# A static instruction order replanned: bank turns, two-row-half score products, work moved between VectorE, GpSimdE and ScalarE, and identity products in early pauses

## The chip, the cores and the metric

One core of one Trainium2 chip. The metric is the device time of one execution in microseconds (us). Engines are called by the profile's names: PE (TensorE's products), DVE (VectorE), ACT (ScalarE), POOL (GpSimdE) and SP (which issues the transfers here).

## The reference

Three stages in float32, one after the other:

```python
# 1: attention, 2 batches x 8 heads x 768 positions x 64; a row keeps 8 global and 96 local keys
scores = q @ k.T / 8 - slope[h] * dist;  a = softmax(where(keep, scores, -1e9));  x = a @ v
# 2: 1536 tokens, 512 -> 2048 -> 512
h = x @ w_in
g = (a0 + a1*h + a2*h**2 + a3*h**3) / (1 + |b0|*|h| + |b1|*h**2 + 1e-6);  x = g @ w_out
# 3: 512 -> 1024 -> 512
h = x @ w_in2;  s = h * softmax(h);  out = (layernorm(s) * g_ln) @ w_out2
```

## The kernel before

**The plan.** `record` (line 300) writes the whole program down as small operations, each with an engine, a planned duration (`lat`), the time after which its engine is free (`occ`) and what it reads and writes. `Plan.run` (202) then simulates the engines at build time: whenever an engine is free it takes the operation whose due time (worked back from the end, less a `lead`) is earliest, and the instructions are issued in just that order. At run time each engine executes its list in order and waits on semaphores. So a wrong planned duration costs nothing by itself, but puts an instruction at a place in its queue where it may hold up what stands behind it. `lock=True` marks operations that want the memory port which DVE and POOL share.

**Attention.** 48 units, each 128 queries of two heads; 128 keys for the first tile of a batch (n=1), else 256 (n=2). `u_load` (390) brings q/k and v by SP. `u_front` (398): scores on PE (lines 405-406, both heads into two halves of one PSUM bank; q is padded with zeros, so that each product runs over all 128 rows), score plus bias and row maximum on DVE (411), exp on ACT (418), reciprocal on DVE (423-424), scaling by it on POOL (429). `u_back` (438): transposes on PE (446), copy out on ACT (458), the product with v on PE (453, the two heads in two 64-column halves of the array), results split in a high and a low part on ACT (460) and DVE (82).

**Second stage.** Four blocks of 384 tokens, 64 steps in five segments, of 8, 16, 16, 16 and 8 steps. The attention of block 0 (12 units) stands ahead of step 0; that of block 1 is recorded in steps 0 to 7, of block 2 in 8 to 22, of block 3 in 24 to 38 (`UW`). A step makes one 128x384 h by 12 products (`h_mm`, lines 574-580), g by a chain of ACT and DVE operations that all use h's bank (`e_ops`, 600-619, its last one on POOL), and three steps later 9 products into the y banks (`y_mm`, 665-671).

**Weights.** 48 pieces, of 512 KB as 64-bit floats, are loaded by SP (485) and rebuilt as float32 by integer operations (`w_conv`): ACT scales (509), POOL reduces the high word to its sign (526, "signs"), DVE shifts and joins (530, 518). The form without "signs" exists in the code as `bits`, two DVE operations (513-514), but `ZS = range(48)` selects "signs" for all. `w_split` makes a high part (ACT, 548) and a low one (POOL, 549, shown as L82). Pieces 0 to 31 are of stage 2, 32 to 47 of stage 3.

**Third stage.** 12 tiles: transposes (731), 24 products into two banks (750-752, tag "h2"), the softmax and norm chain on DVE and ACT (772-794), transposes of its result (812, "lT"), their copies (820, 82), 24 products (834-836, "o"), output.

**Bias.** `bias_pair` (367): eight DVE operations that stand between the first units' maxima.

Of the kernel before, what the change touches and what calls it, by code (L numbers as in the profile page):

```python
# [30 lines left out]
UW = {1: (0, 7), 2: (8, 15), 3: (24, 15)}  # L31
# [3 lines left out]
M2 = (41, 22)  # L35

ZS = range(48)
# [3 lines left out]
WLEAD = 2.0  # L41


SLOW = (5.0, 1.2)
# [82 lines left out]
class Plan:  # L127
# [4 lines left out]
    SEM = 0.05  # L132
# [54 lines left out]

    def settle(self, n):
# [13 lines left out]
    def run(self, emit=True):  # L202
        self.deadlines()
        self.pools = {p: [(0.0, s) for s in sl] for p, sl in self.slots.items()}
        for v in {v for o in self.ops for v in o.vals}:
            v.left, v.free = len(v.users), 0.0
# [18 lines left out]
        while left:  # L225
            best = None
            for e, l in ready.items():
                c = []
                for o in l:
                    t = max(o.t0, at[e])  # L230
                    ok = True
                    need = {}
                    for v in o.new:
# [3 lines left out]
                        need[v.pool] = need.get(v.pool, 0) + 1  # L237
                        fr = self.pools[v.pool]
                        if self.line[v.line][x][0] is not v or len(fr) < need[v.pool]:
                            ok = False  # L240
                            break
                        t = max(t, sorted(fr)[need[v.pool] - 1][0])
                    if ok:
                        if o.lock:
                            t = max(t, port)
                        c.append((t, o))
# [18 lines left out]
            at[e] = t + o.occ  # L265
            o.end = t + o.lat
            if o.lock:
                port = t + o.occ
            if e == "SP":
                dma = max(dma, at[e]) + o.move  # L270
                o.end = dma + o.lat
            for v in o.vals:
                v.left -= 1
# [14 lines left out]
def fast_path(tc, const, qkv, w_in, w_out, w2_in, w2_out, coef, g_sb, nv, ident, out):  # L288
# [3 lines left out]
    plan.settle(ROUNDS)  # L292
    with tc.manual_schedule():
        plan.run()
# [5 lines left out]
def record(tc, es, const, qkv, w_in, w_out, w2_in, w2_out, coef, g_sb, nv, ident, out):  # L300
# [29 lines left out]
    op = P.op  # L330
# [22 lines left out]
    def bias_keep():  # L353
# [26 lines left out]
    xs = {}  # L380
# [9 lines left out]
    def u_load(u):  # L390
        u.qk, u.v = Val("qk"), Val("v")
        w = 256 + u.w
        uop("SP", 2.0, lambda: sync.dma_start(out=qkt[u.qk.slot][:, 0:w], in_=qkv[u.t, u.p, :, 0:w]), occ=0.4,
            new=[u.qk], move=0.8, tag="ld")
        uop("SP", 2.0, lambda: sync.dma_start(out=vt[u.v.slot][:, 0:u.w], in_=qkv[u.t, u.p, :, w:w + u.w]), occ=0.4,
            new=[u.v], move=0.4, tag="ld")

    def u_front(u, bank):
        u.s, u.e, u.st = Val(bank), Val("e"), Val("st")
        w, b0, n = u.w, 0 if u.first else 8, u.w // 128  # L400

        def qk():
            a = qkt[u.qk.slot]
            for h in range(2):
                pe.matmul(out=pb[:, u.s.slot, h * 256:h * 256 + w], lhsT=a[:, h * 128:(h + 1) * 128],  # L405
                          rhs=a[:, 256:256 + w], start=True, stop=True)

        def smax():
            e, st = et[u.e.slot], stt[u.st.slot]
            for h in range(2):  # L410
                dve.tensor_tensor_reduce(out=e[:, h, 0:w], in0=pb[:, u.s.slot, h * 256:h * 256 + w],  # L411
# [778 lines left out]
```

## Time and profile before

| | us |
|---|---|
| median of 3 runs (568.31 to 568.39) | 568.36 |
| the profiled execution's own time | 569.23 |
| its span, first to last instruction | 567.4 |
| PE busy in the span | 529.6 (93%) |
| DVE busy | 429.2 (76%) |
| ACT busy | 390.2 (69%) |
| POOL busy | 223.9 (39%) |

The profiled execution took 0.87 us more than the median of the runs. Busy time is the union of an engine's instructions; a share of the whole span hides that the stages differ, so the stages are read one by one. PE's ends are modelled, so that a short pause between two of its products can count as busy.

### The profile page before, as it was taken

How to read it: one execution, taken by the hardware profiler on the slowest of the kernel's cores; microseconds unless marked ns; L12 is line 12 of the kernel's file. 1: busy time of each engine (PE TensorE's matmuls, PEld its weight loads, DVE VectorE, ACT ScalarE, POOL GpSimd, SP SyncE). 2: the span in 40 equal slices, each digit the busy share in tenths (PEclk: the TensorE clock that was granted, in tenths of full speed). 3: DMA queues.
4: the chain of work that ended last, by engine and by line, in shares of the span. 5: the costliest groups of instructions: out<-in, count | busy, mean ns of one | idle time of the engine just before them, and what ended most of it. 6: DMA issues, size and time to landing. Idle time of an engine off the chain costs nothing.

```text
span 567.4 us, 8749 instructions
## 1 busy us (share of the span) xinstructions
PE 529.6 (93%) x2808; PEld 437.8 (77%) x2808; DVE 429.2 (76%) x1045; ACT 390.2 (69%) x903; POOL 223.9 (39%) x278
## 2 busy tenths in 40 slices
PE   4899998999989899999999989998999999999985
PEld 2567887878877688888887877877878888888865
DVE  6777888998999997677679999889866555555540
ACT  4788888898988888777788887877634444433331
POOL 3675456546677743332335563756400000000000
PEclk9999999999999999999999999999999999999989
DMA  7779255533444443110043230233001111000001
GB/s 247 244 259 324 89 167 161 165 102 94 130 160 152 134 133 114 36 58 26 2 149 130 75 115 34 76 111 104 25 21 39 40 54 37 22 35 20 18 20 43
DMA packets 28278, 56.24 MB, mean 99 GB/s; under 512 B 3520, under 2 KB 11968, under 8 KB 28224
## 3 DMA queue, kind: packets, MB, share of 16 engines
q1 hardware_dynamic: 28080, 55.59, 30.0%
q8 instruction: 24, 0.39, 0.3%
q14 instruction: 30, 0.25, 0.1%
q10 hardware_dynamic: 144, 0.00, 0.0%
HBM read 47.72 MB, written 7.86 MB: 98 GB/s over the span
## 4 chain that ended last, share of the span: by engine, by line
PE 51%; DVE 27%; ACT 15%; issue 4%; POOL 1%; DMA 1%; ACTq 0%; SPq 0%; POOLq 0%; DVEq 0%
PE pb L834 4%; PE pb L836 4%; PE pb L835 4%; PE pb L405 4%; PE pb L750 4%; PE pb L752 4%; PE pb L751 4%; DVE t L615 3%; DVE t L604 3%; DVE t L602 3%; PE pb L453 3%; PE pb L574 3%; PE pb L665 3%; PE pb L580 3%; DVE t L613 3%
## 5 line engine op out<-in xcount | busy, mean ns | idle before, releaser
L82 POOL TENSOR_TENSOR g<-t,g 128x384 fp32r<-128x384 f32 x64 | 69.4, 1084 | 79.9 <-ACT g L617 74.2
L574 PE MATMUL pb<-x,w 128*128 128x384 f32 x256 | 90.0, 352 | 5.4 <-DVE t L607 5.2
L576 PE MATMUL pb<-x,w 128*128 128x384 f32 x256 | 86.2, 337 | 0.0
L665 PE MATMUL pb<-w,g 128*128 128x512 f32 x192 | 78.3, 408 | 7.4 <-ACT g L617 6.3
L429 POOL TENSOR_SCALAR e<-e,st 128x256 f32<-128x256 f32 (+1 forms) x96 | 47.3, 505 | 75.0 <-DVE st L424 56.1
L666 PE MATMUL pb<-w,g 128*128 128x512 f32 x192 | 76.2, 397 | 0.0
L82 POOL TENSOR_TENSOR w<-wst,w 128x512 fp32r<-128x512 f32 x48 | 64.7, 1354 | 18.8 <-ACT w L548 16.2
L574 PEld LDWEIGHTS pb<-x,w 128*128 128x128 f32 x256 | 48.2, 188 | 14.0 <-DVE t L607 10.7
L580 PE MATMUL pb<-x,w 128*128 128x384 f32 x256 | 57.5, 346 | 0.0
L671 PE MATMUL pb<-w,g 128*128 128x512 f32 x192 | 57.2, 406 | 0.0
L405 PE MATMUL pb<-qk 128*128 128x256 f32 (+1 forms) x192 | 50.0, 392 | 6.7 <-DMA qk<-in_qkv 5.4
L602 DVE TENSOR_TENSOR t<-t,pb 128x384 f32<-128x384 f32 x64 | 35.1, 548 | 22.3 <-ACT t L603 20.8
L418 ACT ACTIVATE e<-e,st 128x256 f32<-128x256 f32 (+1 forms) x96 | 46.3, 486 | 5.3 <-DVE st L411 5.1
L665 PEld LDWEIGHTS pb<-w,g 128*128 128x128 f32 x192 | 36.3, 189 | 17.4 <-ACT g L617 9.3
L580 PEld LDWEIGHTS pb<-x,w 128*128 128x128 f32 x256 | 44.7, 188 | 6.2 <-issue 2.4
L576 PEld LDWEIGHTS pb<-x,w 128*128 128x128 f32 x256 | 48.3, 189 | 1.3
L405 PEld LDWEIGHTS pb<-qk 128*128 128x128 f32 x192 | 35.4, 208 | 12.9 <-DMA qk<-in_qkv 5.4
L606 ACT ACTIVATE pb<-pb 128x384 f32<-128x384 f32 x64 | 30.4, 476 | 20.9 <-DVE t L604 20.6
L600 ACT ACTIVATE t<-pb,coef 128x384 f32<-128x384 f32 x64 | 42.6, 666 | 2.6 <-PE pb L580 1.6
L617 ACT CAST g<-t 128x384 fp32r<-128x384 f32 x64 | 32.7, 512 | 16.9 <-DVE t L615 10.6
L607 DVE SCALAR_TENSOR_TENSOR t<-pb,coef,t 128x384 f32<-128x384 f32 x64 | 39.2, 612 | 6.8 <-ACT pb L606 6.1
L615 DVE SCALAR_TENSOR_TENSOR t<-t,coef,t 128x384 f32<-128x384 f32 x64 | 42.7, 667 | 0.7
(106 smaller groups left out, 1261.6 us busy)
## 6 DMA issues: line engine op xcount, KB each, us to landing
wst<-in_w_in SPq DMA_DIRECT2D x24, 512.0 KB, 4.3
wst<-in_w_out SPq DMA_DIRECT2D x24, 512.0 KB, 4.1
qk<-in_qkv SPq DMA_DIRECT2D x40, 256.0 KB, 3.2
v<-in_qkv SPq DMA_DIRECT2D x40, 128.0 KB, 2.5
y_d<-y SPq DMA_DIRECT2D x12, 256.0 KB, 2.7
y<-y_d SPq DMA_DIRECT2D x12, 256.0 KB, 2.6
out<-wst SPq DMA_DIRECT2D x11, 256.0 KB, 2.0
qk<-in_qkv SPq DMA_DIRECT2D x8, 192.0 KB, 3.3
```

The lines of the kernel that those rows point to most:

```text
L82: eng.tensor_tensor(out=out, in0=a, in1=hi.bitcast(F32), op=ALU.subtract)
L405: pe.matmul(out=pb[:, u.s.slot, h * 256:h * 256 + w], lhsT=a[:, h * 128:(h + 1) * 128], rhs=a[:, 256:256 + w], start=True, stop=True)
L418: act.activation(out=e[:, h, 0:w], in_=e[:, h, 0:w], func=AF.Exp, scale=-1.0, bias=st[:, h:h + 1], accum_out=st[:, 2 + 2 * h:3 + 2 * h])
L429: pool.tensor_scalar(out=e[:, h, 0:w], in0=e[:, h, 0:w], scalar1=st[:, 6 + h:7 + h], scalar2=0.0, op0=ALU.mult, op1=ALU.add)
L574: pe.matmul(out=pb[:, g.h.slot, 0:n], lhsT=wt[wh.slot][:, cs[p]], rhs=xt[x[p][0].slot][:, 0:n], start=(p == 0), stop=False)
L576: pe.matmul(out=pb[:, g.h.slot, 0:n], lhsT=wt[wl.slot][:, cs[p]], rhs=xt[x[p][0].slot][:, 0:n], start=False, stop=False)
L580: pe.matmul(out=pb[:, g.h.slot, 0:n], lhsT=wt[wh.slot][:, cs[p]], rhs=xt[x[p][1].slot][:, 0:n], start=False, stop=(p == 3))
L602: op("DVE", 0.14 + 0.41 * k, lambda: dve.tensor_tensor(out=T(g.c), in0=T(g.c), in1=h(), op=ALU.mult), r=[g.h], w=[g.c], tag="ch")
L615: op("DVE", 0.15 + 0.41 * k, lambda: stt_(out=T(g.c), in0=T(g.c), scalar=coef[:, 0:1], in1=T(g.b), op0=ALU.add, op1=ALU.mult), r=[g.b], w= ...
L665: pe.matmul(out=pb[:, y[i].slot, :], lhsT=gt[g.gh.slot][:, c], rhs=wt[wh.slot], start=g.first, stop=False)
L666: pe.matmul(out=pb[:, y[i].slot, :], lhsT=gt[g.gh.slot][:, c], rhs=wt[wl.slot], start=False, stop=False)
L671: pe.matmul(out=pb[:, y[i].slot, :], lhsT=gt[g.gl.slot][:, c], rhs=wt[wh.slot], start=False, stop=g.last)
```

## The change

- `Plan.run`: an operation on a PSUM bank may start only when the last operation on that bank, if it was another engine's, has ended; waits for the shared port lengthen the waiting operation instead of putting it back; an operation that needs two buffers of a pool can claim them. Planned durations, occupancies and start times are changed, and a table `LEADS` moves the due times of operations by tag.
- Scores of blocks 0 and 3 are made over 64 rows per head instead of 128 (`START = ('hh',)`, `TWO = (3,)`), into two banks instead of two halves of one.
- The scaling of 19 units (`NDVE`), the low part of 6 weights (`WDVE`) and 22 of the 48 "signs" (`ZS`, replaced by a second DVE operation) go from POOL to DVE. The eight bias operations go from DVE to ACT, with one DVE operation more ahead of them.
- Weights 16 to 31 are recorded over steps 8 to 22 instead of 6 to 14, those of stage 3 over 17 steps instead of 22; a load waits for the last h product recorded before it (`after`).
- In the first 30 planned microseconds, where PE is planned to pause, products of the identity with itself are put into an unused bank (`fill`).

```diff
-UW = {1: (0, 7), 2: (8, 15), 3: (24, 15)}
+UW = {1: (0, 7), 2: (8, 15), 3: (25, 14)}
-M2 = (41, 22)
-ZS = range(48)
+WS = (8, 14)
+M2 = (41, 17)
+ZS = (2, 4, 6, 8, 10, 12, 15, 17, 18, 20, 22, 24, 26, 28, 30, 32, 33, 34, 35, 36, 38, 40, 42, 44, 46, 47)
-SLOW = (5.0, 1.2)
+SLOW = (5.0, 0)
+START = ('hh',)
+TWO = (3,)
+NDVE, WDVE = (3, 4, 5, 6, 7, 8, 9, 10, 11, 14, 15, 36, 38, 39, 40, 41, 42, 44, 46), (11, 20, 31, 42, 44, 45)
+LEADS = {"o": -35.2, "ld": 41.4, "h2": 1.9, "norm": -0.8, "ex": -9.6, "wg": -18.1, "q": 0.2, "xcp": 0.6, "wld": -0.8, "yev": 9.0, "bias": -2.2, "ln": -1.0, "gl": -7.5, "yT": -12.1, "abs": -0.9, "wbits": -0.1, "pv": 0.0, "ch2": -0.5, "n3": 1.3, "lT": -8.0, "wlo": 0.5, "sq": -5.0, "tre": 10.0, "n2": -1.1, "xh": -0.2, "whi": 2.5, "xl": -0.7, "wzs": -1.6, "y": -0.4}
+BEGIN = {"PE": 2.0, "ACT": 5.0, "DVE": 3.4, "POOL": 1.0, "SP": 1.6, "X": 0.0}
+BANKS = ("h", "s", "p", "y0", "y1", "y2")
+FILL = (30.0, 0.45, 0.25)
...
+                    for v in o.vals:
+                        if v.pool in BANKS and v.last is not None and v.last.eng != e:
+                            t = max(t, v.last.end + self.SEM)
...
-            at[e] = t + o.occ
-            o.end = t + o.lat
+            wait = max(0.0, port - t - self.PORT) if o.lock else 0.0
+            at[e] = t + o.occ + wait
+            o.end = t + o.lat + wait
...
+                if e == "PE" and fill and t < FILL[0]:
+                    spare = [b for p in ("y2", "y1", "y0", "p") for f, b in self.pools[p] if f <= idle and b not in [v.slot for v in o.vals if v.pool in BANKS]]
+                    fill(int((t - idle - 0.1) / FILL[2 if idle > BEGIN["PE"] else 1]), spare)
...
+    def fill(n, spare):
+        for _ in range(n if spare else 0):
+            nc.tensor.matmul(out=plan.pb[:, spare[0], 0:128], lhsT=ident, rhs=ident, start=True, stop=True)
...
-        dve.tensor_scalar(out=kp, in0=kp, scalar1=-1.0, scalar2=-MASK, op0=ALU.add, op1=ALU.mult)
+        dve.tensor_scalar(out=kp, in0=kp, scalar1=-1.0, scalar2=MASK * 256, op0=ALU.add, op1=ALU.mult)
+        dve.tensor_tensor(out=dz, in0=dz, in1=kp, op=ALU.add)
     def bias_pair(p):
         for h in (2 * p, 2 * p + 1):
-            dve.scalar_tensor_tensor(out=bt[h], in0=dz, scalar=-8.0 * SLOPE[h], in1=kp, op0=ALU.mult, op1=ALU.add)
+            act.mul(bt[h], dz, -8.0 * SLOPE[h])
...
+        two, ndve = len(bank) == 2, u.k in NDVE
...
+        def score(h):
+            return pb[:, u.s[h].slot, 0:w] if two else pb[:, u.s[0].slot, h * 256:h * 256 + w]
...
-                pe.matmul(out=pb[:, u.s.slot, h * 256:h * 256 + w], lhsT=a[:, h * 128:(h + 1) * 128],
-                          rhs=a[:, 256:256 + w], start=True, stop=True)
+                r = slice(h * 64, (h + 1) * 64) if two else slice(0, 128)
+                pe.matmul(out=score(h), lhsT=a[r, h * 128:(h + 1) * 128], rhs=a[r, 256:256 + w], start=True, stop=True)
...
-                pool.tensor_scalar(out=e[:, h, 0:w], in0=e[:, h, 0:w], scalar1=st[:, 6 + h:7 + h],
-                                   scalar2=0.0, op0=ALU.mult, op1=ALU.add)
+                (dve if ndve else pool).tensor_scalar(out=e[:, h, 0:w], in0=e[:, h, 0:w], scalar1=st[:, 6 + h:7 + h],
+                                                      scalar2=0.0, op0=ALU.mult, op1=ALU.add)
...
-        op("POOL", 1.27, lambda: minus(nc, pool, wt[lo.slot], src(), wt[hi.slot]), r=[st, hi], w=[lo], lock=True, lead=WLEAD, tag="wlo")
+        if nlo[0] - 1 in WDVE:
+            op("DVE", 0.68, lambda: minus(nc, dve, wt[lo.slot], src(), wt[hi.slot]), r=[st, hi], w=[lo], lock=True, lead=WLEAD, tag="wlo")
...
-            w_make(wseq[made[0]])
+            w_make(wseq[made[0]], [gs[-1].op] if gs else [])
...
-            make_to(2 * s + 4)
+            make_to(min(2 * s + 4, max(2 * SEGS[0][2], 2 * SEGS[0][2] + (s - WS[0]) * (32 - 2 * SEGS[0][2]) // WS[1])))
...
-            w_make(w2seq[made2])
+            w_make(w2seq[made2], [gs[-1].op])
```

## Rows read from the trace of the kernel before

**Rows 1.** Busy time by stretch: us of the stretch, its length, then for each engine busy us (instructions), the granted clock of PE, the share of the DMA engines and GB/s. Block 0's attention; steps 0 to 23; steps 24 to 39; steps 40 to 63 and the first tile of stage 3; the end.
```profile
0.00:45.20 45.20, 32.81 (x183) 22.36 (x184) 32.95 (x142) 31.22 (x98) 27.09 (x51) 0.96 0.75 247
45.20:190.00 144.80, 137.92 (x801) 114.05 (x800) 131.38 (x328) 126.55 (x313) 87.72 (x109) 0.99 0.48 156
190.00:287.40 97.40, 96.67 (x550) 81.04 (x550) 74.68 (x196) 76.99 (x184) 38.33 (x49) 1.00 0.21 62
287.40:416.40 129.00, 120.21 (x576) 102.21 (x575) 115.20 (x202) 100.55 (x199) 70.80 (x70) 1.00 0.27 90
...
543.40:567.40 24.00, 15.19 (x89) 12.96 (x87) 4.33 (x10) 4.78 (x12) 0.00 (x0) 0.88 0.11 37
```

**Rows 2.** Waits over the span: who waited, for whom, us in total, times, longest. Operations 602 and 603 read the same h bank and share no other tile; 600, 603 and 606 are ACT's, 602, 604 and 607 DVE's.
```profile
DVE t L602 <- ACT t L603: 20.8, 20, 2.5
DVE t L604 <- ACT t L603: 3.4, 6, 0.7
SPq L485 <- POOL w L82: 85.2, 29, 9.7
```

**Rows 3.** The same view for 190 to 287 us (first row) and for 287 to 416 us (the others).
```profile
DVE t L602 <- ACT t L603: 15.4, 11, 2.5
...
PE pb L574 <- DVE t L607: 4.0, 6, 1.2
DVE t L602 <- ACT t L603: 2.8, 5, 0.9
```

**Rows 4.** Timeline of DVE: the same operations where they met no POOL operation, and where they did.
```profile
31.43 0.17 DVE L423 TENSOR_SCALAR st<-st 128x2 f32<-128x2 f32 x1
163.32 0.55 DVE L611 SCALAR_TENSOR_TENSOR t<-t,t 128x384 f32<-128x384 f32 x1
165.12 0.92 DVE L423 TENSOR_SCALAR st<-st 128x2 f32<-128x2 f32 x1
171.78 1.32 DVE L611 SCALAR_TENSOR_TENSOR t<-t,t 128x384 f32<-128x384 f32 x1
```

**Rows 5.** Groups of DVE by line in 45.2 to 190 us, columns: count, busy us, mean ns of one, idle time before them.
```profile
L611 DVE SCALAR_TENSOR_TENSOR t<-t,t 128x384 f32<-128x384 f32 x21 | 14.4, 685 | 0.1
L423 DVE TENSOR_SCALAR st<-st 128x2 f32<-128x2 f32 x22 | 9.8, 446 | 0.5 <-ACT e L418 0.5
```

**Rows 6.** Groups of instructions by line with their shapes over the span, columns as in Rows 5.
```profile
L369 DVE SCALAR_TENSOR_TENSOR bt<-t,t 128x264 bf16<-128x264 f32 x8 | 3.1, 422 | 0.0
L365 DVE TENSOR_SCALAR t<-t 128x264 f32<-128x264 f32 x1 | 0.3, 298 | 0.0
L530 DVE SCALAR_TENSOR_TENSOR pb<-pb,wst 128x512 int32<-128x512 int32 x48 | 33.2, 691 | 3.5 <-POOL wst L526 3.5
L526 POOL TENSOR_SCALAR wst<-wst 128x512 f32<-128x512 f32 x48 | 34.3, 715 | 12.1 <-ACT pb L509 7.2 <-PE pb L580 1.6
L429 POOL TENSOR_SCALAR e<-e,st 128x256 f32<-128x256 f32 x80 | 40.6, 520 | 64.4 <-DVE st L424 53.9 <-ACT t L610 3.9 <-PE pb L446 2.2
L82 POOL TENSOR_TENSOR w<-wst,w 128x512 fp32r<-128x512 f32 x48 | 64.7, 1354 | 18.8 <-ACT w L548 16.2 <-PE pb L671 1.3 <-PE pb L446 0.3
L82 DVE TENSOR_TENSOR ll<-pb,lh 128x512 fp32r<-128x512 f32 x24 | 16.5, 686 | 17.3 <-ACT lh L820 17.3
```

**Rows 7.** Busy time by stretch, as in Rows 1, within block 0's attention.
```profile
5.40:20.00 14.60, 11.24 (x42) 7.59 (x42) 12.43 (x54) 8.31 (x28) 7.44 (x12) 1.00 0.82 284
26.00:29.20 3.20, 3.20 (x15) 2.37 (x15) 2.31 (x8) 1.92 (x6) 2.01 (x4) 0.50 0.34 112
```

**Rows 8.** Timeline of PE in block 0's attention: start, us that the merged instructions took together, line, tiles, how many.
```profile
15.48 0.70 PE L453 MATMUL pb<-pt,v 128*64 128x128 f32 x4 [0.52 <-ACT pt L458]
22.22 0.44 PE L453 MATMUL pb<-pt,v 128*64 128x128 f32 x4
26.66 1.92 PE L405 MATMUL pb<-qk 128*128 128x256 f32 x4
30.86 1.03 PE L405 MATMUL pb<-qk 128*128 128x256 f32 x4
31.92 0.66 PE L453 MATMUL pb<-pt,v 128*64 128x128 f32 x8
32.53 0.89 PE L446 MATMUL pb<-ident,e 128*128 128x128 f32 x4
```

**Rows 9.** Busy time by stretch, as in Rows 1: a stretch around step 20, and tile 10's output products after PE's pause.
```profile
168.90:172.70 3.80, 3.20 (x8) 2.63 (x9) 3.73 (x7) 3.36 (x7) 3.17 (x4) 0.55 0.44 138
547.00:551.30 4.30, 4.08 (x14) 3.27 (x15) 1.45 (x3) 0.59 (x1) 0.00 (x0) 0.63 0.01 4
```

**Rows 10.** Timeline at the end of stage 3: DVE's last operation on tile 10's result; the start of tile 9's output products; transposes of tiles 10 and 11.
```profile
534.35 0.81 DVE L794 TENSOR_SCALAR wst<-wst,st 128x1024 f32<-128x1024 f32 x1
...
537.94 0.39 PE L834 MATMUL pb<-w,lh 128*128 128x512 f32 x1
543.44 1.04 PE L812 MATMUL pb<-ident,wst 128*128 128x128 f32 x8
547.22 0.66 PE L812 MATMUL pb<-ident,wst 128*128 128x128 f32 x4 [2.74 <-DVE wst L794]
554.82 0.60 PE L812 MATMUL pb<-ident,wst 128*128 128x128 f32 x4
555.65 0.39 PE L834 MATMUL pb<-w,lh 128*128 128x256 f32 x1 [0.24 <-ACT wst L843]
```

More of the change, by code (lines that the diff above doesn't have):

```diff
@@ L186, in deadlines, with late @@
             o.due = t
+    def late(self, d, o):
+        return self.SEM + (0.05 if o.eng == "POOL" else 0.0) + (0.1 if d.eng == "POOL" and o.eng == "PE" else 0.0)
     def settle(self, n):
@@ L200, in settle, with run @@
         return best[0]
-    def run(self, emit=True):
+    def run(self, emit=True, fill=None):
         self.deadlines()
@@ L205, in run @@
         for v in {v for o in self.ops for v in o.vals}:
-            v.left, v.free = len(v.users), 0.0
+            v.left, v.free, v.last = len(v.users), 0.0, None
         todo = [len(o.deps) for o in self.ops]
@@ L212, in run @@
         ready = {e: [] for e in ("PE", "ACT", "DVE", "POOL", "SP", "X")}
-        at = {e: 0.0 for e in ready}
+        self.begin, at = BEGIN, dict(BEGIN)
         head = {p: 0 for p in self.line}
-        port, dma = 0.0, 0.0
+        port, dma, idle = 0.0, 0.0, BEGIN["PE"]
         def add(o):
-            o.t0 = max((d.end for d in o.deps), default=0.0) + self.SEM
+            o.t0 = max((d.end + self.late(d, o) for d in o.deps), default=0.0)
             ready[o.eng].append(o)
@@ L236, in run @@
                         x = head[v.line] + sum(y.line == v.line for y in o.new[:o.new.index(v)])
-                        need[v.pool] = need.get(v.pool, 0) + 1
-                        fr = self.pools[v.pool]
-                        if self.line[v.line][x][0] is not v or len(fr) < need[v.pool]:
+                        if self.line[v.line][x][0] is not v:
                             ok = False
                             break
-                        t = max(t, sorted(fr)[need[v.pool] - 1][0])
+                        need[v.pool] = need.get(v.pool, 0) + 1
+                    if not ok:
+                        continue
+                    for p, k in need.items():
+                        fr = self.pools[p]
+                        if len(fr) < k:
+                            ok = False
+                            if k > 1:
+                                claims[p] = min(claims.get(p, 1e9), o.due - o.lead)
+                        else:
+                            t = max(t, sorted(fr)[k - 1][0])
                     if ok:
-                        if o.lock:
-                            t = max(t, port)
-                        c.append((t, o))
+                        c.append((max(t, port - self.PORT) if o.lock else t, o, need))
+            for e, c in can.items():
+                c = [(t, o) for t, o, need in c if all(o.due - o.lead <= claims.get(p, 1e9) + CLAIM for p in need)]
                 if not c:
@@ L264, in run @@
             o.start = t
-            at[e] = t + o.occ
-            o.end = t + o.lat
+            wait = max(0.0, port - t - self.PORT) if o.lock else 0.0
+            at[e] = t + o.occ + wait
+            o.end = t + o.lat + wait
             if o.lock:
-                port = t + o.occ
+                port = o.end - (self.PORT2 if e == "POOL" else self.PORT)
             if e == "SP":
@@ L271, in run @@
                 o.end = dma + o.lat
+            o.prev = [v.last for v in o.vals if v.pool in BANKS and v.last is not None]
             for v in o.vals:
+                v.last = o
                 v.left -= 1
@@ L292, in fast_path @@
     plan.settle(ROUNDS)
+    def fill(n, spare):
+        for _ in range(n if spare else 0):
+            nc.tensor.matmul(out=plan.pb[:, spare[0], 0:128], lhsT=ident, rhs=ident, start=True, stop=True)
     with tc.manual_schedule():
-        plan.run()
+        plan.run(True, fill)
     for cm in held:
@@ L484, in w_load @@
         n = 1024 if wide else 512
[L485 to L486 removed]
+        op("SP", 2.0, lambda: sync.dma_start(out=wst[st.slot][:, 0:n], in_=src.bitcast(I32)), occ=0.42, new=[st],
+           move=2.0, after=after, tag="wld")
         return st
[L489 removed]
+    nconv, nlo = [0], [0]
     def w_conv(st, new=()):
```

98 lines of the change are left out of this document (52 added, 46 removed).

## The prediction

> **What bounds it now.** I read the busy time by stretch first [rows 1], because the page's one share for PE, 93%, mixes stages. Three stages give time away. While block 0's attention runs alone (0 to 45.2 us) no engine is above 73%: PE 32.8, DVE 33.0 of 45.2, so a chain of latencies bounds it, not an engine. In steps 0 to 23 DVE is busy 131.4 of 144.8 us and PE pauses 6.9; in steps 40 to 63 DVE is busy 115.2 of 129.0 and PE pauses 8.8. There DVE is nearest to being the bound. Steps 24 to 39 are PE's: 96.7 of 97.4. At the end PE pauses 8.8 of 24.0.
>
> The view of waits came second. DVE's first operation of a step, 602, waits 20.8 us in all for ACT's 603, and 604 waits 3.4 for it [rows 2]. 602 and 603 share only the h bank: the program makes engines take turns on a bank, and the old plan has no entry for that, so it puts 602 behind an ACT operation it cannot see. But 15.4 of the 20.8 us lie in steps 24 to 39, where PE does not pause; 2.8 lie in steps 40 to 63, beside 4.0 us of PE waiting on the same chain [rows 3]. Knowing the turns is worth little by itself.
>
> Third, the durations. DVE's 423 takes 0.17 us alone and 0.92 beside a POOL operation, 611 takes 0.55 and 1.32 [rows 4]; in steps 0 to 23 the means are 446 and 685 ns [rows 5]. Times the counts, 22 x 0.28 + 21 x 0.135 = 9.0 us of DVE's busy time there is waiting for POOL.
>
> **What moves between engines.** Of the 48 conversions 22 lose POOL's 715 ns and get a second DVE operation like 530, 691 ns: +15.2 us on DVE. 19 units' scaling leaves POOL (2 x 520 ns); on DVE no row has it, the nearest is 365 on 264 columns, 298 ns. Bounds 0.15 (half of it) to 0.5 (DVE no better than POOL) each; I take 0.27, 0.54 per unit, +10 us. Six low parts leave POOL (1354 ns); DVE's nearest is 686 ns: +4.1. The bias leaves DVE (-3.1, plus about 0.4 for the new operation) and costs ACT eight operations, 3.4 at DVE's own 422 ns, in a stage where ACT has 14 us to spare [rows 1, 6]. Altogether DVE gets 26 to 27 us more, and POOL some 43 less. Split by stage: block 0 +5 (5 conversions, 9 units, bias off), steps 0 to 23 +11.4 (12 conversions 8.3, 3 low parts 2.1, 2 units 1.0), block 3's units +4, steps 40 to 63 +5.5 (5 conversions, 3 low parts).
>
> **Block 0: -5 us.** Four products of line 453 still take 0.70 us at 15.48, but 0.44 at 22.22; four of 405 take 1.92 at 26.66, in a stretch with granted clock 0.50, the 1.2 GHz level, and 1.03 at 30.86 at 2.4 GHz [rows 7, 8]. So PE runs slow until about 20 us and again for 3.2 us, though the clock column reads 1.00 at first. With identity products in the pauses it should rise early and not fall: 11.24 us of products to 20 us become about 7.1, 3.2 become 1.6, 5.8 us less PE work [rows 7]. PE is busy in 73% of the stage, but beside DVE and ACT as busy as that; I count half of the 5.8 as on the path, 3 us. The bias off DVE's path to the first maxima: 1 us of its 3.1. Two row halves save a quarter of 1.03 (below) for twelve units, 3.1, half of it on the path: 1.5. DVE's scaling skips a hand-over to POOL and back: 0.5. Against it +5 us of DVE work with 12 us idle; I let 1 through. Bounds: +5 (all of it exposed, the rest hidden) to -12.4 (PE never pauses).
>
> **Steps 0 to 23: -0.5 us.** DVE needs 131.4 + 11.4, less a share of the port waits: POOL sheds 12 x 0.715 + 3 x 1.354 + 2 x 1.04 = 14.7 of its 87.7 us, 17%, so 1.5 of 9.0 [rows 1, 5, 6]. That is 141.3. At the 98% that DVE reaches in its densest stretch (3.73 of 3.80) [rows 9] it takes 144.2, against 144.8 now. Bounds -3.5 (no idle at all) to +9.9 (the added work in full). The loads now wait for an h product; behind a waiting load on SP stand q/k, v and x transfers, but loads already wait 85.2 us for staging buffers [rows 2], and q/k loads get a lead of 41 us, so I price it at 0; without that cover a late q/k would stop PE.
>
> **Steps 24 to 39: -3 us.** PE is the bound, so PE work saved is time. Block 3 has 12 units, whose 405 takes 1.03. Nothing in this trace splits rows; columns are split in 453: four products take 0.44, eight 0.66 instead of 0.88, three quarters [rows 8]. By that 12 x 1.03 x 0.25 = 3.1. Bounds: 0 and half, 6.2. The Trainium skill (TensorEngine Tiling (Array Packing), Overview, Theoretical Speedup) gives up to 2x for a contraction of 64; by it this term would be 6.2, and the trace's 453 does not reach that. The same page (Tiling Modes, Key Properties) says that a change of tiling mode drains the engine, which speaks against 24 units that change it once more; the trace has 446 start 0.61 us after the eight products of 453 [rows 8], with no drain beyond their own time, so by this row the sum stays. DVE gets +4 with 22.7 idle: hidden.
>
> **Steps 40 to 63: -2.5 us.** DVE 115.2 + 5.5 = 120.7; at 98% 123.2, -5.8, if the order is as dense as that. 602's 2.8 and part of 604's 3.4 should go with the turns in the plan, so I take under half. Bounds -5.8 to +5.5.
>
> **The end: -3.5 us.** Tile 10's result is there at 535.2, but PE does tile 9's output products first, from 537.94; transposes come at 543.44, PE then sits 2.74 us for tile 11, and the second half of tile 11's transposes waits behind tile 10's output until 554.82 [rows 10]. The pause costs twice: the clock averages 0.63 in the following 4.3 us [rows 9]. With lead -35.2 for "o" and -8.0 for "lT", transposes go first: 0.9 us of them at 537.9, both output groups of 5.5 us to 549.8, tile 11's transposes to 550.7, copies of 1.4, and the last group at 552.1 instead of 555.65. Bounds 0 and -4.4 (half of PE's 8.8 us).
>
> **Sum.** -5 - 0.5 - 3 - 2.5 - 3.5 = -14.5. The profiled execution's 569.23 (its span of 567.4 and 1.83 around it) becomes 554.7. It stands 0.87 above the median of the runs, so the median becomes 553.9.
>
> **Rivals.** (a) The order closes more: block 0 -10, then -3.5, -6.2, -5.8, -4.4, together -29.9: 538.5. For it: DVE and ACT are only 70% busy in block 0, and the old plan knew neither the turns nor the longer durations beside POOL [rows 2, 4]; against: DVE needs 141.3 of the 144.8 us of steps 0 to 23, which leaves no room there.
> (b) DVE becomes the bound. In steps 0 to 23 the second conversion operation stands on DVE between operations of the g chain; if each delays it, +9.9 there and +5.5 later, with block 0 unchanged and -3 and -3.5 kept: +8.9, 577.3. It decides once over 6.5 of these 15.4 us are exposed, which is what row halves and end give. For it: DVE's 97% need; against: 13.4 us of DVE idle time there that a better order could fill [rows 1]. The Trainium skill (SBUF - State Buffer, Who interferes with whom) says that whoever holds the port shared by the two blocks the other for its whole instruction; DVE's scaling and low parts are such operations, and the 0.92 and 1.32 us agree [rows 4].
> (c) The change doesn't do what it says: the pauses that the plan sees are not those on the chip, so identity products stand ahead of products that are ready (ten pauses of about 0.25 us, -2 left of block 0), row halves run one after the other, and nothing else moves: 566.
>
> **Chances.** Forecast 0.50 (its own range 545 to 562), (a) 0.20, (b) 0.15, (c) 0.10, all terms cancelling 0.05. A measurement of this kernel can tell 0.2%, 1.1 us. Faster: 0.50 + 0.20 + 0.10 = 0.80; same 0.05; slower 0.15. The range 538 to 568 leaves out (b) and about 0.05 below it.
>
> **What would show it.** Right: step 0's first product (now at 45.2) near 40; four products of 453 at about 0.44 from the first on, no clock of 0.50 before 30 us; block 3's 405 near 0.77 per four; DVE over 95% in steps 0 to 23 with PE's pauses no larger; no pause over 1 us at the end before tile 11. Wrong: DVE's busy time in steps 0 to 23 up by 11 us with the stretch longer; 405 still at 1.03; 423 still at 446 ns; identity products followed at once by late scores.

## The result

The changed kernel takes 558.71 us, median of four runs (558.11 to 560.19), against 568.38 of the kernel before on the same chip: ratio 0.9833, 95% interval 0.9812 to 0.9855, so 9.7 us or 1.7% faster. Forecast were 553.9 us and -14.5. The profiled execution took 558.11, its span is 556.3 us instead of 567.4: -11.1. That is more than 9.7 because the execution profiled before took 0.9 us more than its median and this one 0.6 less. By stage it is

| stage | before | after | change | forecast |
|---|---|---|---|---|
| block 0's attention, to the first product of step 0 | 45.3 | 43.7 | -1.6 | -5 |
| steps 0 to 23 | 146.9 | 147.7 | +0.7 | -0.5 |
| steps 24 to 39 | 95.2 | 93.1 | -2.1 | -3 |
| steps 40 to 63 | 127.1 | 121.3 | -5.7 | -2.5 |
| from there to the end | 152.9 | 150.6 | -2.3 | -3.5 |

(Stages run from the first h product of a step, and from the last step's first y product, in the timelines; lengths are rounded.) The sign is right, and the end and steps 24 to 39 came near. Block 0 gave a third of its term, and the largest gain is in steps 40 to 63. A list can put attention work of later blocks on either side of a stage's border, so a stage's length is read beside PE's busy time in it.

### The profile page after: what moved, and what is told of

It is laid out like the page before. It is cut to its first block, busy times and chain, and to the rows that moved or that the text cites. A ratio compares the mean times of both kernels' runs of the same rounds, so it can differ in the third digit from the quotient of the medians.

```text
span 556.3 us, 8937 instructions
## 1 busy us (share of the span) xinstructions
PE 531.8 (96%) x2910; PEld 437.0 (79%) x2910; DVE 446.0 (80%) x1104; ACT 393.0 (71%) x911; POOL 182.5 (33%) x212
## 3 DMA queue, kind: packets, MB, share of 16 engines
HBM read 47.72 MB, written 7.86 MB: 100 GB/s over the span
## 4 chain that ended last, share of the span: by engine, by line
PE 55%; DVE 29%; ACT 10%; issue 4%; DMA 1%; POOL 0%; SPq 0%; ACTq 0%; DVEq 0%; POOLq 0%
PE pb L894 4%; PE pb L896 4%; PE pb L895 4%; PE pb L634 4%; PE pb L810 4%; PE pb L812 4%; PE pb L811 4%; PE pb L640 4%; PE pb L731 3%; PE pb L636 3%; PE pb L725 3%; DVE t L667 3%; PE pb L459 3%; DVE wst L574 3%; PE pb L726 3%
## 5 line engine op out<-in xcount | busy, mean ns | idle before, releaser
L99 POOL TENSOR_TENSOR w<-wst,w 128x512 fp32r<-128x512 f32 x42 | 57.2, 1364 | 42.7 <-ACT w L604 38.8
L482 POOL TENSOR_SCALAR e<-e,st 128x256 f32<-128x256 f32 (+1 forms) x58 | 28.0, 495 | 54.4 <-DVE st L477 48.4
L669 ACT ACTIVATE t<-t,coef 128x384 f32<-128x384 f32 x64 | 39.6, 618 | 6.8 <-DVE t L667 6.6
L662 DVE TENSOR_TENSOR t<-t,pb 128x384 f32<-128x384 f32 x64 | 35.2, 549 | 11.1 <-ACT t L663 6.5
L677 ACT CAST g<-t 128x384 fp32r<-128x384 f32 x64 | 32.8, 512 | 16.0 <-DVE t L675 15.3
L880 ACT CAST lh<-pb 128x512 fp32r<-128x512 f32 x24 | 13.9, 592 | 42.5 <-PE pb L872 42.5
L459 PE MATMUL pb<-qk 64*128 64x256 f32 (+3 forms) x192 | 41.3, 393 | 2.7 <-DVE st L464 1.0
L671 DVE SCALAR_TENSOR_TENSOR t<-t,t 128x384 f32<-128x384 f32 x64 | 40.6, 634 | 1.3 <-ACT t L670 1.3
```

Of the source, the lines that this page charges most:

```text
L99: eng.tensor_tensor(out=out, in0=a, in1=hi.bitcast(F32), op=ALU.subtract)
L459: pe.matmul(out=score(h), lhsT=a[r, h * 128:(h + 1) * 128], rhs=a[r, 256:256 + w], start=True, stop=True)
L671: op("DVE", 0.15 + 0.41 * k, lambda: stt_(out=T(g.a), in0=T(g.a), scalar=1.0 + 1e-6, in1=T(g.b), op0=ALU.add, op1=ALU.mult), r=[g.b], w=[g ...
```

## The profile after

Old line numbers become new ones thus: 405 to 459 (scores), 453 to 509, 423 to 476, 429 to 482 (scaling), 530 to 570 and 586, 574 to 634 (first h product), 602 to 662, 603 to 663, 607 to 667 (DVE's last reading of an h bank), 611 to 671, 617 to 677 and 665 to 725 (g and the y product that needs it), 794 to 854, 812 to 872, 834 to 894, 82 to 99; the identity products are line 337.

Busy time by stretch, columns as in [rows 1]: block 0 whole, block 0 from 13 us on, steps 0 to 23, 24 to 39, 40 to 63.
```profile
0.00:43.70 43.70, 39.16 (x291) 29.41 (x291) 34.54 (x155) 30.39 (x102) 11.03 (x25) 1.00 0.62 200
13.00:43.70 30.70, 28.98 (x224) 20.73 (x223) 28.10 (x114) 23.46 (x78) 7.64 (x9) 1.00 0.58 183
...
43.70:191.30 147.60, 140.33 (x810) 113.03 (x808) 140.60 (x355) 132.41 (x323) 81.45 (x98) 1.00 0.54 172
191.30:284.40 93.10, 92.93 (x534) 74.49 (x535) 79.47 (x208) 74.42 (x179) 26.11 (x30) 1.00 0.20 61
284.41:405.72 121.31, 117.27 (x570) 101.74 (x569) 113.56 (x202) 98.78 (x194) 61.29 (x58) 1.00 0.29 94
```
The same view of the kernel before for stretches that [rows 1] does not have: block 0 from 13 us on, and exactly steps 0 to 23 (the stretch in [rows 1] ends 2.2 us ahead of step 24) and 40 to 63.
```profile
13.00:45.20 32.20, 27.45 (x164) 18.71 (x164) 24.78 (x95) 25.81 (x81) 23.20 (x36) 0.95 0.76 252
...
45.28:192.22 146.94, 139.93 (x816) 115.43 (x814) 132.64 (x331) 128.60 (x317) 89.47 (x111) 0.99 0.48 155
...
287.45:414.50 127.05, 118.64 (x571) 101.27 (x569) 113.67 (x197) 100.29 (x198) 70.80 (x70) 1.00 0.27 91
```
The third busy column is DVE. In steps 0 to 23 it has 140.60 us instead of 132.64 and fills 95% of the stage, and the stage is no shorter. In block 0 from 13 us on it is busy 28.10 of 30.70 us, 92%, where it was 24.78 of 32.20. In steps 40 to 63 its load is what it was, and PE pauses 4.0 us where it paused 8.4.

The two stretches of [rows 7] again: the second had a granted clock of 0.50 and now has 1.00.
```profile
5.40:20.00 14.60, 13.43 (x103) 10.70 (x103) 10.82 (x49) 10.78 (x36) 4.75 (x9) 1.00 0.77 267
26.00:29.20 3.20, 3.20 (x26) 2.13 (x25) 3.13 (x18) 2.55 (x11) 0.00 (x0) 1.00 0.35 112
```

Timeline of PE in block 0, as [rows 8]; x4 counts the profile's instructions, for 459 and 509 two for each product of the program.
```profile
12.01 0.44 PE L509 MATMUL pb<-pt,v 128*64 128x128 f32 x4 [0.33 <-ACT pt L514]
...
31.87 0.70 PE L459 MATMUL pb<-qk 64*128 64x256 f32 x4
32.50 0.66 PE L509 MATMUL pb<-pt,v 128*64 128x128 f32 x8
...
35.60 1.03 PE L459 MATMUL pb<-qk 128*128 128x256 f32 x4
36.56 0.66 PE L509 MATMUL pb<-pt,v 128*64 128x128 f32 x8
```
The first four output products already take 0.44 us, which before was reached at 22.22 only: PE runs at its upper level from its first score at 5.42 on. The identity products ahead of that took 0.24 us each (2.93 for 12), those behind it 0.13 (2.39 for 19). Four scores in row halves take 0.70 us where full rows take 1.03, and a product of line 509 behind them starts 0.63 after their start, not 0.96.

Groups of DVE, columns as in [rows 5]: two in steps 0 to 23 (43.7 to 191.3 us), then the scaling over the span.
```profile
L671 DVE SCALAR_TENSOR_TENSOR t<-t,t 128x384 f32<-128x384 f32 x21 | 14.6, 694 | 0.0
L476 DVE TENSOR_SCALAR st<-st 128x2 f32<-128x2 f32 x22 | 3.5, 161 | 0.1
```
```profile
L482 DVE TENSOR_SCALAR e<-e,st 128x256 f32<-128x256 f32 x36 | 12.1, 379 | 0.4
```
476 hardly meets a POOL operation any more (161 ns, it was 446); 671 still does (694, it was 685). The scaling's mean of 379 ns is made of 35 operations of 0.35 us and one of 1.38, which met a POOL operation; I had taken 0.27.

Waits over the span, as [rows 2]: the two at which PE stands longest on the chain from h to g, and DVE's for ACT at an h bank.
```profile
PE pb L725 <- ACT g L677: 4.2, 7, 1.0
PE pb L634 <- DVE t L667: 1.8, 3, 0.8
...
DVE t L662 <- ACT t L663: 6.5, 8, 1.7
DVE t L662 <- ACT t L660: 4.4, 7, 0.8
```
DVE's 20.8 us for 603 became 6.5. PE's two were 6.3 and 5.2.

Timeline at the end of stage 3, as [rows 10].
```profile
531.93 0.81 DVE L854 TENSOR_SCALAR wst<-wst,st 128x1024 f32<-128x1024 f32 x1
...
537.21 1.03 PE L872 MATMUL pb<-ident,wst 128*128 128x128 f32 x8
538.05 0.50 PE L894 MATMUL pb<-w,lh 128*128 128x512 f32 x1
...
544.50 0.39 PE L894 MATMUL pb<-w,lh 128*128 128x256 f32 x1 [0.68 <-ACT wst L903]
```
All transposes of tile 11 (537.21) stand ahead of tile 10's output products, and the pause of 2.74 us ahead of them is gone; what is left is 0.68 us ahead of tile 11's own output products.

## The experiments

My theory was the prediction's: parts with a price each, which add up. The rival: the kernel is its order, so that a part undone changes everything behind it and its price can't be read. Three edits keep the order, or nearly so, and are told first. "Count" below is the end that the planner computes for its own list from its own durations. It is no time of the chip; the span less the count says how honest the list is. Ratios are to the kernel before on the same chip, whose median was 568.6 to 568.95.

**No identity products**, same order otherwise.
```diff
-        plan.run(True, fill)
+        plan.run(True)
```


> The changed kernel (558.7) without the identity products; the order of all other instructions is the same. Theory 1, the prediction's: they keep PE at 2.4 GHz through block 0's attention, worth 3 us; without them four products of the line with v take 0.70 us again up to about 20 us, step 0 starts at about 46.7 instead of 43.7, and the time is 561 to 562. Theory 2: block 0 is bound by DVE's and ACT's chain and PE's clock there is hidden; step 0 stays within 0.7 us of 43.7 and the time is 558.7 to 559.4.

Measured 560.38 us, ratio 0.9854 (0.9828 to 0.988). Only block 0 changed, 43.66 to 45.91: the identity products give 2.25 us, nearer to the first theory's 3 than to the second's 0.7; the run's time lies between their ranges. Its PE timeline shows the lower level again, 0.70 and 1.43 where the changed kernel has 0.44 and 0.70:
```profile
11.99 0.70 PE L509 MATMUL pb<-pt,v 128*64 128x128 f32 x4 [0.52 <-ACT pt L514]
...
18.63 1.43 PE L459 MATMUL pb<-qk 64*128 64x256 f32 x4 [1.50 <-DVE st L464]
```

**No row halves**, same order and banks.
```diff
-                r = slice(h * 64, (h + 1) * 64) if two else slice(0, 128)
+                r = slice(0, 128)
```


> The changed kernel with the scores of blocks 0 and 3 made over all 128 rows again, in the same order and into the same two banks. Theory 1: block 3's twelve units lie where PE is the bound, four products take 0.87 instead of 0.63, so 12 x 0.235 = 2.8 us there and up to 1.5 in block 0: 561.5 to 563. Theory 2: the halves save PE work that other engines' waits take back: under 1 us, 558.7 to 559.7.

Measured 560.53, 0.9852 (0.9831 to 0.9874). Block 0 is 1.7 us longer and steps 24 to 39 are 1.1 longer, the other stages equal within 0.1: 2.8 us by stages, 2.6 in the span. Here too the run's time lies between the two ranges, for the 2.8 us expected in steps 24 to 39 are 1.1.

By their ratios these two runs stand only 1.2 and 1.1 us above the changed kernel, inside its interval. It is the stages, equal within 0.1 us where nothing was changed, that show the rest.

**The kernel before with four of the new leads.**
```diff
+LEADS = {"o": -35.2, "lT": -8.0, "yT": -12.1, "h2": 1.9}
-        ... o.lead, ... = ... lead, ...
+        ... o.lead, ... = ... lead + LEADS.get(tag, 0.0), ...
```


> The kernel before with the new leads of stage 3 alone (o -35.2, lT -8.0, yT -12.1, h2 1.9). The prediction: transposes go ahead of output products at the end, the stage from step 63's last product to the end falls from 152.9 by 2 to 3.5 us, to 149.4 to 151, the time to 565 to 566.4. Rival: the order at the end comes from the corrected durations of the softmax chain, not from the leads: 152.5 to 153.5, 568.4.

Measured 566.23, 0.9957 (0.994 to 0.9973). All stages to step 63 keep their length, and the end goes from 152.9 to 150.4: the whole of the changed kernel's gain there, as the prediction said. Its last group has the same pause of 0.68:
```profile
552.93 0.39 PE L835 MATMUL pb<-w,lh 128*128 128x256 f32 x1 [0.68 <-ACT wst L844]
```

These three give 2.25 + 2.8 + 2.5 = 7.5 of the 11.1 us of the spans. What is left lies in the turn rule, the durations and the moves between engines, all of which change the order.

**The kernel before with the turn rule alone.**
```diff
+                    for v in o.vals:
+                        if v.pool in BANKS and v.last is not None and v.last.eng != e:
+                            t = max(t, v.last.end + self.SEM)
```


> The kernel before (568.4) with one thing added: its plan knows the turns on a PSUM bank; no instruction is added or moved to another engine. Theory R, the rule carries the gain: steps 40 to 63 shrink by 3 to 6 us and the time is 560 to 565. Theory L, the gain of the changed kernel hangs on its whole tuned order, of which the rule is only one part: within 3 us of 568.4, either way. The prediction's own view was that the rule is worth under 2.5 us: 566 to 568.

Measured 566.34, 0.9956 (0.9938 to 0.9974). As the prediction held (566 to 568), the rule alone is worth little. Steps 24 to 39 fell by 4.5, steps 0 to 23 rose by 2.4, steps 40 to 63 by 0.7. Most of the 4.5 is work that moved: PE is busy 3.9 us less in steps 24 to 39 and 2.7 more in steps 0 to 23. DVE's wait for ACT at the h bank only fell from 20.8 to 15.3 us, and PE's waits for g rose:
```profile
PE pb L670 <- ACT g L622: 9.2, 8, 2.8
...
PE pb L579 <- DVE t L612: 5.1, 9, 0.8
...
DVE t L607 <- ACT t L608: 15.3, 19, 2.1
```

**The changed kernel without the turn rule** (those three lines removed, planned anew).

> The changed kernel with a plan that does not know of the turns on a PSUM bank (planned anew, all else kept). Theory 1: the first DVE operation of a step waits for ACT's third one again (6.5 us in all now, about 20 then), of which only the few us in steps 40 to 63 and 0 to 23 count: +1 to +3, 560 to 562. Theory 2: the turns are what the new order lives on: +5 or more, over 563.5.

Measured 571.4, 1.0052 (1.0032 to 1.0071): slower than the kernel before. Steps 40 to 63 take 132.7 instead of 121.3. The rule alone gives 2.5 us, and without it the rest of the change loses all of its gain: it is no part with a price of its own. How much of the 12.7 us is the rule and how much another list, the runs after the next one tell.

**The changed kernel without the moves** (planned anew).
```diff
-ZS = (2, 4, 6, 8, ...)
-NDVE, WDVE = (3, 4, 5, ...), (11, 20, ...)
+ZS = range(48)
+NDVE, WDVE = (), ()
```


> The changed kernel with the 22 second conversion operations, the 19 scalings and the 6 low parts back on POOL (planned anew). Theory 1, the prediction's account of DVE: it loses 26 us of work in stages where it is the nearest to being the bound, so steps 0 to 23 and 40 to 63 get shorter by up to 4 us together and block 0 longer by 0.5: 555 to 559. Theory 2: POOL's operations hold up DVE and the chain behind them by more than their work on DVE costs; DVE's two-column add before the reciprocal goes from 163 ns back to over 300, steps 0 to 23 grow by 3 to 8 us: 562 to 567.

Measured 562.55, 0.9895 (0.9869 to 0.9921). Block 0 is 1.8 us shorter than in the changed kernel, steps 24 to 39 6.6 shorter, steps 0 to 23 10.9 longer. Of the last two, some 6 us are again work moved over the border: PE is busy 146.5 us instead of 140.4 in steps 0 to 23 and 86.5 instead of 92.9 in steps 24 to 39. Together the two stages are 4.4 us longer. That can be the moves or another list. Two runs say how much a list weighs:

**One planned constant moved**, 0.05 to 0.06 (a hand-over of POOL's port) and 0.04 to 0.045 (a semaphore), nothing else.
```diff
-    SEM, PORT, PORT2 = 0.04, 0.02, 0.05
+    SEM, PORT, PORT2 = 0.04, 0.02, 0.06
```


> The changed kernel with one planned duration altered by 10 ns (PORT2 0.05 to 0.06 us); no rule, engine or instruction is changed, only the order that comes out of the plan. Theory R: such a change moves little, 557.5 to 560.5. Theory L: orders from one set of rules scatter, and the leads were fitted to one of them: 561 to 568.

> The changed kernel with the planned semaphore time 0.045 instead of 0.04 us, nothing else: a second order from the same rules. Theory R: 557.5 to 560.5. Theory L: 561 to 568.

Measured 563.92, 0.9921 (0.9905 to 0.9938), and 566.92, 0.9976 (0.9964 to 0.9988). Moving one planned constant by 10 ns costs 5 us, another by 5 ns 8 us, half of the gain and more. Both fall on the slow side; the leads were fitted to the changed kernel's own list, so a list planned anew starts with that handicap whatever else was undone. So the replanned runs above resolve nothing under some 8 us. The run without the moves, 3.8 us slower, shows nothing of them. The run without the turn rule, 12.7 us slower, lies 4 us and more beyond both. The waits of the second:
```profile
PE pb L725 <- ACT g L677: 8.7, 9, 3.4
PE pb L634 <- DVE t L667: 2.9, 4, 1.9
```

**The moves undone in the unchanged order.** Where that order has a DVE operation of the 19 scalings, six low parts and 22 conversions, POOL gets the old one; the engines' lists are otherwise the same.
```diff
-                (dve if ndve else pool).tensor_scalar(out=e[:, h, 0:w], ...
+                pool.tensor_scalar(out=e[:, h, 0:w], ...
...
-            dve.scalar_tensor_tensor(out=a, in0=a, scalar=3, in1=w1, ...
-            dve.scalar_tensor_tensor(out=a, in0=w1, scalar=0x7FFFFFFF, in1=a, ...
+            signs()
+            shift()
...
-            op("DVE", 0.68, lambda: minus(nc, dve, ...
+            op("DVE", 0.68, lambda: minus(nc, pool, ...
```


> The changed kernel with its order and banks kept instruction for instruction, but the 19 units' scaling, the six low parts and the second operation of the 22 conversions are given to POOL again, each issued at its old place in the order. Theory 1 (the moves carry a gain of their own: they take POOL off the port that it shares with DVE): DVE sheds some 25 us, but the DVE add before the reciprocal goes back from 163 ns to over 250, hand-overs to POOL come back in block 0 (nine units, two each), so block 0 is 1 to 3 us longer, steps 0 to 23 3 to 8 us, in all +5 to +10, 564 to 570. Theory 2 (DVE is nearest to the bound, and work taken off it gives time back): within 2 us of the changed kernel or below it, 557 to 562. The replanned run without the moves (562.6) could not tell them apart, since its whole order was another.

Measured 574.0, 1.0091 (1.0072 to 1.0111): 15 us above the changed kernel and beyond both theories' ranges (the profiled execution took 576.0). Steps 0 to 23 and 40 to 63 of it, and two of its waits:
```profile
44.60:201.70 157.10, 143.91 (x812) 113.85 (x809) 131.37 (x334) 132.69 (x322) 94.04 (x117) 0.99 0.52 163
...
295.50:423.30 127.80, 119.48 (x570) 102.72 (x569) 110.23 (x194) 98.92 (x194) 67.41 (x66) 0.99 0.28 90
```
```profile
DVE pb L585 <- POOL wst L581: 28.8, 22, 2.0
...
PE pb L724 <- ACT g L676: 7.9, 8, 2.2
```
DVE has 9.2 us less work in steps 0 to 23 than in the changed kernel, and the stage is 9.4 us longer. All 22 conversions now stop DVE until POOL is done, 28.8 us. In this order a DVE operation of 0.69 us is cheaper than standing behind POOL. It is an upper bound of the moves' worth, since the order was made for them; the replanned 3.8 us, with the scatter of the lists on it, is the other end.

**Other leads, found by the count alone.** Two searches over leads of the changed kernel, and one over the kernel without the turn rule, each kept the list with the lowest count; nothing else changed.
```diff
-LEADS = {"o": -35.2, "ld": 41.4, "h2": 1.9, ...
+LEADS = (20 to 36 other values)
```


> The changed kernel with other leads for 25 kinds of operation, found by a search over leads alone that kept the list with the earliest end in the planner's own count: 547.2 instead of 551.7 us (a count, no measured time). So far the spans of lists made with the turn rule and the new durations stood 3 to 8 us above that count (the changed kernel 4.6, the two with one constant moved 4.2 and 7.9, without the moves between engines 3.3), of lists without the rule 16 to 24 above. Theory 1 (with the turn rule the count is honest, so that it can choose an order): span 550 to 555, run 552 to 558, at or below the changed kernel. Theory 2 (the changed kernel's order is one lucky one, which only runs on a chip could have found): a new order falls like the two with one constant moved, 563 to 567.

> As the run before, from another seed of the search: 20 leads changed, count 548.8 us. Theory 1: span 552 to 557, run 554 to 559, not above the changed kernel by more than 1 us and some 1.5 above the other seed's. Theory 2: 563 to 567.

> The changed kernel without the turn rule in its planner (all else kept: durations, moves, identity products, row halves), and its leads searched in the same way, with the count at 544.2 us instead of 553.4. Theory 1 (without the rule the count leaves out waits that the chip has): the span stands 16 us or more above the count, 560 or more, run 562 to 571, with DVE waiting on ACT at the h banks, and it is slower than both searches with the rule although its count is 3 to 4.6 us lower. Theory 2 (any count will do if one searches enough): 544 + 5, run 551, the fastest of the four.

| list | count | span | span less count | run | ratio (95%) |
|---|---|---|---|---|---|
| before | 543.1 | 567.4 | 24.3 | 568.38 | 1 |
| before, with the turn rule alone | 547.5 | 565.1 | 17.6 | 566.34 | 0.9956 (0.9938 to 0.9974) |
| changed kernel | 551.7 | 556.3 | 4.6 | 558.71 | 0.9833 (0.9812 to 0.9855) |
| one constant 10 ns more | 556.7 | 560.9 | 4.2 | 563.92 | 0.9921 (0.9905 to 0.9938) |
| another 5 ns more | 555.6 | 563.5 | 7.9 | 566.92 | 0.9976 (0.9964 to 0.9988) |
| without the moves | 557.9 | 561.2 | 3.3 | 562.55 | 0.9895 (0.9869 to 0.9921) |
| other leads, first seed | 547.2 | 566.3 | 19.1 | 568.31 | 1.0002 (0.9983 to 1.0021) |
| other leads, second seed | 548.8 | 555.0 | 6.3 | 556.83 | 0.9793 (0.9773 to 0.9813) |
| no turn rule, as changed | 553.4 | 569.8 | 16.4 | 571.4 | 1.0052 (1.0032 to 1.0071) |
| no turn rule, other leads | 544.2 | 571.5 | 27.3 | 573.4 | 1.0083 (1.0063 to 1.0103) |

Without the rule a lower count made a slower kernel, and the wait that the count leaves out stands in the trace:
```profile
PE pb L631 <- DVE t L664: 10.1, 16, 1.3
...
DVE t L659 <- ACT t L660: 15.5, 20, 2.1
```
That half of the theory holds. The other half, that with the rule the count chooses well, held for one seed and failed for the other. The table says two things more. The rule alone does not make the count honest (17.6), nor does the rest of the change, its durations among it, without the rule (16.4); with both, five of six lists stand 3.3 to 7.9 us above it. And the count foresaw 4.9 and 3.9 us of what the two moved constants cost. The second seed's list beats both kernels, by 0.4% against the changed one with intervals that just touch, so it may be equal. The first is 4.5 us below the changed kernel in the count and 10.0 above it on the chip. Waits of the first seed's list, then of the second's:
```profile
PE pb L634 <- DVE t L667: 9.8, 8, 2.3
```
```profile
PE pb L725 <- ACT g L677: 5.4, 10, 1.4
...
PE pb L634 <- DVE t L667: 1.2, 2, 0.8
```
PE waits 9.8 us for DVE to let go of h banks, where the other lists with the rule and the new durations have 1.2 to 3.8. Which of the count's durations hides that is open. One candidate is the port: two DVE operations of g, 671 and 675, take 709 and 691 ns in the first seed's list on average and 634 and 622 in the changed kernel's, 9.2 us in all. That a search finds the count's own errors is my reading, not shown.

## Why the prediction was right and where it was wrong

**Block 0, -5 forecast, -1.6 measured: the terms for PE held, those for DVE failed.** The clock (3) gave 2.25, the row halves (1.5) gave 1.7; those two alone are 4 us, so the rest of the change, which I had at -0.5, costs 2.3 there. The bias, off DVE, gave nothing (-1): DVE's first row maximum waits for ACT's bias and starts at 7.86 us, where it started at 7.69. DVE's load was not the +5 of which I let 1 through: it rose from 32.95 to 34.54, because four of the stage's eight conversions now stand behind step 0. What I had not priced is the port. Two of the 18 scalings meet a POOL low part and take 1.35 and 1.38 us instead of 0.29 and 0.35, and both stand in the chain that ended last. The first of them, on DVE, POOL and PE:
```profile
19.17 1.55 DVE L482 TENSOR_SCALAR e<-e,st 128x128 f32<-128x128 f32 x2
```
```profile
19.38 1.27 POOL L99 TENSOR_TENSOR w<-wst,w 128x512 fp32r<-128x512 f32 x1 [0.51 <-ACT w L604]
```
```profile
20.78 0.33 PE L502 MATMUL pb<-ident,e 128*128 128x128 f32 x1 [0.94 <-DVE e L482]
```
The 2.1 us of the two are about what is missing. In the two lists where one scaling meets POOL block 0 takes 43.0 and 43.2 us, in the one without moves 41.9. Those are other lists, so it is argued, not shown, that the port is the whole of the 2.3.

**Steps 0 to 23, -0.5 forecast, +0.7 measured: near, by errors that cancel.** DVE was to need 141.3 us and has 140.60; I expected it to fill 98%, it fills 95%. Two terms were off. The added work was counted with the conversions where the old recording had them; the later recording, which is part of the change, puts 26 of them into the stage instead of 21 (before, then after):
```profile
L518 DVE SCALAR_TENSOR_TENSOR wst<-wst,pb 128x512 int32<-128x512 int32 x21 | 14.3, 681 | 0.4
```
```profile
L574 DVE SCALAR_TENSOR_TENSOR wst<-wst,pb 128x512 int32<-128x512 int32 x26 | 17.7, 679 | 0.2
```
A conversion has two operations of some 0.69 us besides the new one, so my 11.4 lacks 6.9 us. Against it, of the 9.0 us that 423 and 611 wait for the port I took off 1.5; by the groups above about 3 are left, 21 x (694 - 550) ns, all at 671, so 6 went. I had scaled the waits with POOL's work, but the order weighs more. With POOL's old work back in the unchanged order, 94.0 us of it, the run with the moves undone has 201 ns at 476, not 446:
```profile
L476 DVE TENSOR_SCALAR st<-st 128x2 f32<-128x2 f32 x22 | 4.4, 201 | 0.6 <-ACT e L471 0.6
```
The Trainium skill (SBUF — State Buffer, Who interferes with whom) says that a DVE instruction with two SBUF inputs contends with a GpSimd instruction that reads SBUF. 671, with two such inputs, agrees: the 11 of its 21 that met no POOL operation took 0.54 to 0.56 us, the longest of the others 1.42. But DVE's 97% was not the price of the moves, as rival (b) has it: the run with them undone has 9.2 us less DVE work there and is 9.4 us slower.

**Steps 24 to 39, -3 forecast, -2.1 measured: the row halves save PE time, but their price was mis-sized.** Undone, they cost this stage only 1.1 us, not 3.1. PE pauses 0.2 us there, so all that is saved is on the path. I took a quarter of 1.03, the length up to the modelled end of the last product. What counts is when the next product starts: behind full rows that is after 0.96 us if it is one of line 509, but after 0.67 if it is one of h or y. And the change to row halves costs time itself. Transposes, scores and h products in the changed kernel, then without row halves:
```profile
220.03 0.60 PE L502 MATMUL pb<-ident,e 128*128 128x128 f32 x4
220.56 0.70 PE L459 MATMUL pb<-qk 64*128 64x256 f32 x4
221.19 0.45 PE L634 MATMUL pb<-x,w 128*128 128x384 f32 x1
221.48 0.34 PE L636 MATMUL pb<-x,w 128*128 128x384 f32 x1
```
```profile
221.61 0.60 PE L502 MATMUL pb<-ident,e 128*128 128x128 f32 x4
222.05 1.03 PE L459 MATMUL pb<-qk 128*128 128x256 f32 x4
222.72 0.52 PE L634 MATMUL pb<-x,w 128*128 128x384 f32 x1
223.09 0.34 PE L636 MATMUL pb<-x,w 128*128 128x384 f32 x1
```
The scores start 0.53 us after the transposes instead of 0.44, and from 502 to 636 it is 1.45 us instead of 1.48. Of the stage's 12 units seven save 0.03 to 0.04 us like this, four with line 509 behind the scores 0.23 each, and one loses 0.18. So the cost of a change, which the prediction saw no sign of in [rows 8], is there: some 0.09 us. The other 1 us of the 2.1 comes with the order and is not resolved. The Trainium skill (TensorEngine Tiling (Array Packing), Theoretical Speedup) gives up to 2x; the measured product is 1.5x, 0.70 against 1.03.

**Steps 40 to 63, -2.5 forecast, -5.7 measured: the step that failed is "Knowing the turns is worth little by itself", and with it the port waits, which my sum had at nothing here.** By itself the rule is worth little: alone on the old kernel it moved this stage by +0.7. But I priced it as 2.8 us of waits that go. With all else changed, the two lists without the rule take 132.7 and 132.4 us here, the six with it 121.1 to 126.6: some 6 us at least, outside the scatter of the lists. DVE's work was to rise by 5.5 us and is 113.56, against 113.67 in the same steps before. The added operations came as counted (five conversions 3.5, three low parts 2.1), but 611, 613 and 615 meet POOL less and shed 5.9 us, 53.8 to 47.9; 613, now 673, most:
```profile
L613 DVE SCALAR_TENSOR_TENSOR t<-t,t 128x384 f32<-128x384 f32 x26 | 19.3, 741 | 0.0
```
```profile
L673 DVE SCALAR_TENSOR_TENSOR t<-t,t 128x384 f32<-128x384 f32 x26 | 15.4, 594 | 0.3
```
About half of the -5.7 belongs to this one list: with a constant moved the stage takes 125.2 and 124.6, 1.9 and 2.5 less than before, near what I forecast. PE's pauses fell by 4.4 of the 5.7 us (127.05 - 118.64 to 121.31 - 117.27), most visibly at g and the h banks: those two waits sum to 6.0 us over the span in the changed kernel (5.9 in the two runs that keep its order) and 6.6 in the second seed's, and to 10.5 to 15.7 in the ten other kernels, the kernel before (11.5) among them. That is a mark that goes with the time, not a measured cause.

**The end, -3.5 forecast, -2.3 measured.** The mechanism is right and shown alone (-2.5 in the kernel before). PE's pauses at the last two tiles fell by 2.06 us (2.74 + 0.24 to 0.24 + 0.68), and the clock no longer falls there. Against it PE now pauses 1.66 us (105.28 - 103.62) in the first 105 us of this stage, where it was 0.57 (105.50 - 104.93), 1.1 more: bringing transposes forward moved part of the wait to an earlier tile (in the kernel before with the four leads it is 1.37). I had counted no new wait.

**Rivals.** (a) did not come: no stage closed as far, but for steps 40 to 63, whose -5.7 is nearly (a)'s own figure. (b) did not come: steps 0 to 23 rose by 0.7 and not by 9.9. (c) is refuted: clock, row halves and pauses are all in the trace. Of my signs, step 0 near 40 us failed (43.66); the clock, 405 at 0.70, DVE at 95% and no pause over 1 us at the end came.

## What to carry to other kernels

In a kernel whose order comes from a planner, a part that changes the order has no price of its own: 10 ns in one planned constant moved it by 5 us and 5 ns in another by 8, so an ablation that plans anew needs such a null run beside it, and one that keeps the order is worth more. A rule that makes the planner see a wait is not worth the wait that it removes; together with durations that are right it decides whether the list that looks best is best, and even then the list has to be run. Work that a change moves is priced in the stage where the change puts it, and with what it meets there: a scaling of 0.35 us took 1.38 beside a POOL operation, on the path. And PE work saved is the time until its next product starts, not the length of the product.

## What the runs showed of the hardware

- The granted clock is 1.00 from 5.3 to 554.9 us in the changed kernel. Before it reads 1.00 in 5.4 to 20 us too, while four products of the output take 0.70 us: the first record of the clock is at 19.05 us there (at 30.59 without the identity products), and the products' own time tells the level.
- DVE's scaling of 128 x 256 elements takes 0.35 us alone, which is above 365's 298 ns on 264 columns [rows 6] and 0.17 less than POOL's 520; the one that met POOL's low part took 1.38.
- Four products on half the rows take 0.70 us instead of 1.03, two thirds and not half. What that saves depends on the neighbours: 0.23 us with a product of line 509 behind them, 0.03 to 0.04 with one of h or y, since the change to row halves puts the scores 0.09 us later behind the transposes.
